# Two expert passes of 576 tokens each become one of 512 and one of 640

## The chip, the cores and the metric

The kernel runs on one core of a Trainium2 chip. The metric is the time of one execution on the device in microseconds (us), median of several runs. The core has a matrix engine (PE, with its weight loads shown as PEld), a vector engine (DVE), a scalar engine (ACT), a general one (POOL) and a queue engine (SP) that issues every transfer of this kernel. Each works through its own program in order, and the engines wait for each other by semaphores.

## The reference

Three layers follow each other: attention with pooled queries, a mixture of four experts, and a gated layer.

```python
# q, k, v: (2 batches, 8 heads, 1152, 64); queries are averaged in pairs, so 576 rows a batch
scores = scale * np.matmul(q_pool, k.transpose(0, 1, 3, 2))
attn = np.exp(scores - max); attn = attn / (attn.sum(-1) + 1e-9)
x = np.matmul(attn, v)                       # (2, 8, 576, 64), laid out as 1152 tokens x 512
...
p = domain_probs / (domain_probs.sum(-1, keepdims=True) + 1e-9)
for e in range(4):                           # w1[e]: 512 x 1024, w2[e]: 1024 x 512
    h = np.maximum(x @ w1[e], 0.0)
    out += p[:, e:e + 1] * (h @ w2[e])
...
g = out @ w_gate; val = out @ w_val          # 512 x 1536 each
return (g * sigmoid(g) * val) @ w_out        # 1152 x 512
```

## The kernel before

**Attention.** A unit is one head and one half (288) of a batch's 576 query rows, so batch 0 is units 0 to 15 and batch 1 units 16 to 31. In a unit PE makes nine blocks of scores (tile `sc`, two products each), which ACT copies to `s`; DVE takes the maximum over the blocks (`acc`); PE turns it (`mt`), DVE reduces it (`top`), PE spreads it again (`m`); DVE and POOL subtract it, ACT takes the exponential, and PE multiplies with the values (`av`). Keys and queries are turned on PE first (`tr` from `kraw` and `qraw`). At the end of a pair of units DVE inverts the sums (`den`), POOL multiplies (`xst`), and the result is split into a high part `xhi` (ACT) and a low part `xlo` (POOL or DVE): every large product is done as three products, high by high, low by high and high by low. In batch 0 the product with the values is done in plain fp32, in batch 1 in three parts too.

**Experts.** `experts(b, ...)` works on one batch of 576 tokens. Per expert it makes 8 hidden blocks of 128 and 4 output blocks of 128. Each is a group in one pair of PSUM banks: tokens 0 to 287 in one bank and 288 to 575 in the other, so a product has 288 columns (tile `ps`, line 864). Pairs `p0` and `p1` alternate. ACT and DVE take a hidden group out (`hhi`, `hlo`), DVE an output group times the probability (`yt` or `yacc`), and POOL adds it (`yacc`). Each piece of weights (128x512) comes by a transfer to `wraw`, and is split into `whi` (ACT) and `wlo` (DVE, and POOL for each second piece of the first pass). The pass of batch 0 runs among the attention of batch 1; the pass of batch 1 comes after it. The gated layer then works on all 1152 tokens, with products of 384 columns (tile `g`) and of 512 (tile `o`).

**Order.** `Plan` decides the order of everything up to the end of the first pass. Each step has a due time in units of one block of scores, an engine, a cost, and the names it reads and writes; `arrange` goes through a simple model of the engines and always takes the ready step with the earliest due time. The constants at the top (`MT`, `SUB`, `EXP`, `E0_START` and so on) are those due times. What follows the first pass is sorted by due time alone or left to the tile framework.

**Probabilities.** `prep_probs` loads the 1152x4 table (`praw`), normalizes it in seven small DVE instructions (`total`, `pn`) and stores it to memory (`pd`), from where rows are spread over the partitions (`pb`) as each expert needs them. It is one step, due at 100:

```python
at(100, "DVE", 1.0, prep_probs)
```

Of the kernel before, what the change touches and what calls it, by code (L numbers as in the profile page):

```python
# [26 lines left out]
MT, TOP, MB, MCOPY = 10.23, 11.11, 11.18, 12.05  # L27
SUB = (11.07, 10.75, 13.58)
EXP = ((13.43, 16.94, 15.82), (12.68, 14.5, 17.57))
HALF_HI = (14.41, 16.21, 16.25)  # L30
HALF_LO = (13.1, 15.0, 17.1)
AV = (17.93, 15.5)
FINISH = (22.33, 24.2)
SHARE = (0.7, 2.54, 2.4, 3.2, 3.7)
COPY, MAX = 0.94, 0.25
PREP_Q, PREP_K = (4.3, 5.58, 0.4), (6.33, -0.27)
SPLIT = (-9.69, -6)
E0_START = 159.71
E0_RATE = 9.69
# [124 lines left out]
def tile_kernel(  # L164
# [20 lines left out]
    W = 288  # L185
    NH = SQ // W
# [21 lines left out]
    hp = moe1.enter_context(tc.tile_pool(name="hp", bufs=FC1))  # L208
# [21 lines left out]
    def prep_probs():  # L230
        praw = const.tile([P, TP, NE], F32, tag="praw", name="praw")
        nc.sync.dma_start(out=praw, in_=probs.rearrange("(p t) e -> p t e", t=TP))
        total = const.tile([P, TP], F32, tag="total", name="total")
# [6 lines left out]
        nc.sync.dma_start(out=pd.rearrange("e (p t) -> p e t", t=TP), in_=pn)  # L240
# [82 lines left out]
    def take_piece():  # L323
# [9 lines left out]
        | dict(vraw=2, wraw=3, whi=2, wlo=2, hhi=FC1, hlo=FC1)  # L333
# [4 lines left out]
    xsts, xts = {}, {}  # L338
# [4 lines left out]
    def split_x(b, j, sl, hi=True, lo=True):  # L343
        if b not in xts:
            xts[b] = [
                xp.tile([P, MC, SQ], F32R, tag=f"x{n}", name=f"x{n}{b}") for n in ("hi", "lo")
            ]
        xhi, xlo = xts[b]
        src = xsts[b][:, j, sl]
        if hi:  # L350
            nc.scalar.activation(out=xhi[:, j, sl], in_=src, func=AF.Copy)
        if lo:
            eng = nc.vector if b else nc.gpsimd
            eng.tensor_tensor(
                out=xlo[:, j, sl], in0=src, in1=xhi[:, j, sl].bitcast(F32), op=ALU.subtract
            )
# [279 lines left out]
    def plan_attention():  # L636
# [55 lines left out]
        due_load_q(1, start)  # L692
        due_k(0, 0, start, "d")
        due_q(0, start, "c")
# [142 lines left out]
        for jj in range(NPAIR, B * NPAIR):  # L837
            t = 4 * KC * jj
            for i in range(2):
                ready = t + 6.7 + KC * i  # L840
# [33 lines left out]
    subs = [slice(s * W, (s + 1) * W) for s in range(NH)]  # L874

    def experts(b, at, due):

        pbs, hs, pss, yts = {}, {}, {}, {}
# [3 lines left out]
        def load_p(e):  # L882
            pbs[e] = yp.tile([P, SQ], F32, tag="pb", name=f"pb{b}_{e}", bufs=1)
            nc.sync.dma_start(
                out=pbs[e], in_=pd[e, b * SQ : (b + 1) * SQ].partition_broadcast(P)
            )

        def products(group, i, s, c, src, first, last):

            if group not in pss:  # L890
                pss[group] = pair(expert_bank(group), "ps")
# [4 lines left out]
        def expert_bank(group):  # L896
            return f"p{(group[0] * (FC1 + MC) + group[1]) % 2}"

        def two(t):
            return t.rearrange("p (s w) -> p s w", s=NH)  # L900
# [6 lines left out]
        def evict_h2(e, f):  # L907
            hl = hp.tile([P, SQ], F32R, tag="hlo", name="hlo")
            nc.vector.scalar_tensor_tensor(
                out=two(hl),  # L910
                in0=pss[e, f][:, :, :W],
                scalar=0.0,
                in1=two(hs[e, f][0]).bitcast(F32),
# [3 lines left out]
            hs[e, f].append(hl)  # L917

        def evict_y(e, o):
            if e == 0 and o == 0:  # L920
                yaccs[b] = acc.tile([P, MC, SQ], F32, tag="acc", name=f"yacc{b}")
            t = yaccs[b][:, o, :]
            if e:
                t = yts[o] = yp.tile([P, SQ], F32, tag="yt", name="yt", bufs=1)
            nc.vector.tensor_tensor(  # L925
                out=two(t), in0=pss[e, FC1 + o][:, :, :W], in1=two(pbs[e]), op=ALU.mult
            )

        def add_y(o):
            y = yaccs[b][:, o, :]  # L930
            nc.gpsimd.tensor_tensor(out=y, in0=y, in1=yts[o], op=ALU.add)  # L931

        for e in range(NE):
# [4 lines left out]
            for f in range(FC1 + 2 * MC):  # L938
                o, part = divmod(f - FC1, 2)
                hidden = f < FC1  # L940
                group = (e, f) if hidden else (e, FC1 + o)
                ps = ("ps", b, *group)
                for s in range(NH):
                    for c in range(MC):
                        if hidden:
                            src = lambda c=c: [x[:, c, :] for x in xts[b]]
                            half = s if b == 0 else 0
                            reads = [("xhi", b, c, half), ("xlo", b, c, half)]
                            uses = [("x", b)]
                            first, last = c == 0, c == MC - 1  # L950
                        else:
                            m = MC * part + c
                            src = lambda e=e, m=m: hs[e, m]
                            reads = [("hh", b, e, m), ("hl", b, e, m)]
                            uses = []
                            first, last = m == 0, m == FC1 - 1
                        at(
                            due(n), "PE", 0.397, products, group, w, s, c, src, first, last,
                            kind="r", reads=reads + [("whi", w), ("wlo", w)],
                            writes=[(*ps, s)] + ([(*ps, 1)] if first and s == 0 else []),  # L960
                            uses=uses + [ps],
                            takes=[(expert_bank(group), ps)] if first and s == 0 else [],
                        )
                        n += 3
                    if s == 0:
                        due_split(w + 1, due(n + SPLIT[0]), due(n + SPLIT[1]))
                w += 1
                if hidden:
                    at(
                        due(n - 1) + 0.35, "ACT", 0.64, evict_h, e, f,  # L970
                        reads=[(*ps, 0), (*ps, 1)], writes=[("hh", b, e, f)], uses=[ps],
                        takes=[("hhi", ("hh", b, e, f))],
                    )
                    at(
                        due(n - 1) + 0.55, "DVE", 0.75, evict_h2, e, f,
# [205 lines left out]
```

## Time and profile before

| what | us |
|---|---|
| median of 3 runs | 921.75 (921.39 to 922.65) |
| the profiled execution | 921.15 |
| its span, first to last instruction | 919.4 |
| PE busy | 884.4 |
| DVE, ACT, POOL busy | 576.6, 462.0, 388.4 |
| mean granted clock of PE | 0.997 |

The profiled execution is 0.6 us below the median, and 1.75 us of it lie outside the span. Busy time of PE is a sum of overlapping records, so a share of 96% tells only where PE is not idle. How fast it goes there is told by the distance from one product to the next.

### The profile page before, as it was taken

What the parts mean: (1) busy time and instruction counts of PE and PEld (TensorE: products, weight loads), DVE (VectorE), ACT (ScalarE), POOL (GpSimd) and SP (SyncE); (2) the same over time, 40 slices, a digit from 0 to 9 for tenths busy, and PEclk for the clock granted to TensorE, in tenths of its full rate; (3) what the DMA queues carried; (4) which work ended last, traced back from release to release, by engine and by line L of the source; (5) the groups of instructions that cost most, each with busy time, mean ns of one, the idle gap of its engine ahead of it and who ended that gap; (6) DMA issues with size and microseconds to landing.
All of it is one profiled execution on the core that took longest, in us unless ns stands there. A gap on an engine that the chain in (4) does not pass through costs nothing.

```text
span 919.4 us, 14986 instructions
## 1 busy us (share of the span) xinstructions
PE 884.4 (96%) x5916; PEld 842.3 (92%) x5916; DVE 576.6 (63%) x883; ACT 462.0 (50%) x786; POOL 388.4 (42%) x266
## 2 busy tenths in 40 slices
PE   4899998999999999999999999999999999999998
PEld 3667777899999999999999999999999999999886
DVE  4678778776667577675664334333468988888800
ACT  4678778877776767666633222232323333333110
POOL 2465657867776796778631000203023333222000
PEclk9999999999999999999999999999999999999999
DMA  5012221323233223111243232323333323223210
GB/s 141 2 41 67 49 74 39 101 71 86 72 84 92 65 73 83 46 59 60 60 148 96 89 95 81 94 88 87 92 93 99 107 70 91 92 77 98 78 69 34
DMA packets 124149, 72.30 MB, mean 79 GB/s; under 512 B 32304, under 2 KB 119344, under 8 KB 124080
## 3 DMA queue, kind: packets, MB, share of 16 engines
q1 hardware_dynamic: 124080, 71.36, 26.7%
q8 instruction: 46, 0.75, 0.3%
q14 instruction: 23, 0.19, 0.1%
HBM read 68.96 MB, written 2.38 MB: 78 GB/s over the span
## 4 chain that ended last, share of the span: by engine, by line
PE 89%; DVE 5%; ACT 3%; issue 2%; DMA 1%; POOL 1%; SPq 0%; DVEq 0%; ACTq 0%; POOLq 0%
PE ps L864 43%; PE g L864 16%; PE av L600 12%; PE o L864 8%; PE sc L494 3%; PE sc L495 3%; DVE acc L522 1%; PE mt L528 1%; ACT s L511 1%; PE tr L438 1%; PE tr L464 1%; DVE kt L456 1%; PE m L550 1%; ACT s L573 1%; DVE s L567 1%
## 5 line engine op out<-in xcount | busy, mean ns | idle before, releaser
L306 ACT ACTIVATE whi<-wraw 128x512 fp32r<-128x512 f32 x128 | 80.4, 629 | 174.6 <-PE ps L864 157.1
L567 POOL TENSOR_TENSOR s<-s,m 128x864 f32<-128x864 f32 x64 | 132.2, 2085 | 76.3 <-ACT m L560 76.2
L864 PE MATMUL ps<-xhi,whi 128*128 128x288 f32 x512 | 153.0, 299 | 0.0
L864 PE MATMUL ps<-hhi,whi 128*128 128x288 f32 x512 | 152.2, 297 | 0.0
L864 PE MATMUL ps<-hhi,wlo 128*128 128x288 f32 x512 | 151.1, 295 | 0.0
L864 PE MATMUL ps<-xhi,wlo 128*128 128x288 f32 x512 | 151.0, 295 | 0.0
L864 PE MATMUL ps<-xlo,whi 128*128 128x288 f32 x512 | 150.9, 295 | 0.0
L864 PE MATMUL ps<-hlo,whi 128*128 128x288 f32 x512 | 150.9, 295 | 0.0
L313 DVE TENSOR_TENSOR wlo<-wraw,whi 128x512 fp32r<-128x512 f32 x96 | 81.9, 853 | 101.1 <-ACT whi L306 101.1
L931 POOL TENSOR_TENSOR yacc<-yacc,yt 128x576 f32<-128x576 f32 x24 | 41.3, 1722 | 187.8 <-DVE yt L925 187.8
L511 ACT ACTIVATE s<-sc 128x576 f32<-128x576 f32 (+1 forms) x160 | 93.5, 600 | 47.6 <-PE sc L495 45.9
L573 ACT ACTIVATE s<-s 128x864 f32<-128x864 f32 x96 | 87.7, 921 | 18.4 <-DVE s L567 13.8
L864 PE MATMUL g<-yhi,wlo 128*128 128x384 f32 x288 | 96.3, 334 | 0.5 <-DVE wlo L313 0.5
L864 PE MATMUL g<-yhi,whi 128*128 128x384 f32 x288 | 96.2, 334 | 0.5 <-ACT yhi L1022 0.5
L864 PE MATMUL g<-ylo,whi 128*128 128x384 f32 x288 | 96.2, 334 | 0.0
L864 PEld LDWEIGHTS ps<-xlo,whi 128*128 128x128 f32 x512 | 96.2, 188 | 0.0
L864 PEld LDWEIGHTS ps<-hlo,whi 128*128 128x128 f32 x512 | 96.1, 188 | 0.0
L864 PEld LDWEIGHTS ps<-hhi,whi 128*128 128x128 f32 x512 | 96.1, 188 | 0.0
L864 PEld LDWEIGHTS ps<-xhi,whi 128*128 128x128 f32 x512 | 96.1, 188 | 0.0
L864 PEld LDWEIGHTS ps<-xhi,wlo 128*128 128x128 f32 x512 | 96.1, 188 | 0.0
L864 PEld LDWEIGHTS ps<-hhi,wlo 128*128 128x128 f32 x512 | 96.1, 188 | 0.0
L494 PE MATMUL sc<-qhi,kt 128*128 128x288 f32 x288 | 88.2, 322 | 4.7 <-ACT s L511 1.9
(94 smaller groups left out, 1950.7 us busy)
## 6 DMA issues: line engine op xcount, KB each, us to landing
wraw<-in_moe_w_dram SPq DMA_DIRECT2D x128, 256.0 KB, 2.7
w<-in_moe_w_gate_dram SPq DMA_DIRECT2D x12, 512.0 KB, 3.9
w<-in_moe_w_val_dram SPq DMA_DIRECT2D x12, 512.0 KB, 3.6
w<-in_moe_w_out_dram SPq DMA_DIRECT2D x12, 512.0 KB, 3.5
qraw<-in_q_dram SPq DMA_DIRECT2D x32, 144.0 KB, 2.4
kraw<-in_k_dram SPq DMA_DIRECT2D x14, 288.0 KB, 3.9
v<-in_v_dram SPq DMA_DIRECT2D x8, 288.0 KB, 4.2
vraw<-in_v_dram SPq DMA_DIRECT2D x8, 288.0 KB, 3.0
```

The lines of the kernel that those rows point to most:

```text
L306: nc.scalar.activation(out=hi, in_=t, func=AF.Copy)
L313: eng.tensor_tensor(out=lo, in0=t, in1=hi.bitcast(F32), op=ALU.subtract)
L438: nc.tensor.matmul(pt[:, m * P : (m + 1) * P], kr[:, c].rearrange("p h d -> p (h d)"), ident, is_transpose=True,)
L456: nc.vector.tensor_tensor(out=kt[other, sl], in0=pt[me, : 3 * P], in1=kt[me, sl].bitcast(F32), op=ALU.subtract)
L494: nc.tensor.matmul(ps, wt, qhi, start=True, stop=False)
L495: nc.tensor.matmul(ps, wt, qlo, start=False, stop=True)
L511: nc.scalar.activation(out=s[:, c : c + n, :], in_=ps[:, :n, :W], func=AF.Copy)
L567: eng.tensor_tensor(out=sg, in0=sg, in1=m.unsqueeze(1).to_broadcast([P, 3, W]), op=ALU.subtract)
L573: nc.scalar.activation(out=sg, in_=sg, func=AF.Exp)
L600: nc.tensor.matmul(avs[u][:, :W], w[:, c].rearrange("p t d -> p (t d)"), e, start=(c == 0 and n == 0), stop=(c == KC - 1 and n == len(term ...
L864: nc.tensor.matmul(ps, w, x, start=first and n == 0, stop=last and n == len(terms) - 1)
L931: nc.gpsimd.tensor_tensor(out=y, in0=y, in1=yts[o], op=ALU.add)
```

## The change

The experts no longer follow the batches. The first pass takes the last 512 tokens of batch 0, as single products of 512 columns. The second takes the first 64 tokens of batch 0 and all of batch 1, 640 tokens, as two products of 320 columns. So the first pass has half as many products: 768 of 512 columns where there were 1536 of 288; the second keeps 1536, of 320 columns. In the first pass a group is now two outputs, one to each bank of a pair, and taken out in one instruction of 1024 columns. The second pass has tiles of its own for the hidden part. The low and high parts of `x` lie in one tile of 640 columns, and the rows of the last layer go to their places in up to two transfers.

The work on the probabilities is three steps (load, normalize, store), placed at 100, 104 and 112. All due times of the plan have other values, and one transposition of queries is written ahead of one of keys.

```diff
-MT, TOP, MB, MCOPY = 10.23, 11.11, 11.18, 12.05
+MT, TOP, MB, MCOPY = 2.7, 9.26, 6.21, 7.32
...
-E0_START = 159.71
-E0_RATE = 9.69
+E0_START = 165.31
+E0_RATE = 9.43
...
+    T0 = 512
+    REST = SQ - T0
+    T1 = NT - T0
...
+    def load_probs():
         praw = const.tile([P, TP, NE], F32, tag="praw", name="praw")
         nc.sync.dma_start(out=praw, in_=probs.rearrange("(p t) e -> p t e", t=TP))
...
-            xhi, xlo = (x[:, subs[s]] for x in src())
-            gemm(pss[group][:, s, :W], [(whi, xhi), (whi, xlo), (wlo, xhi)], first, last)
+            xhi, xlo = src()
+            gemm(pss[group][:, s, :cols], [(whi, xhi), (whi, xlo), (wlo, xhi)], first, last)
...
-        def evict_h(e, f):
-            hh = hp.tile([P, SQ], F32R, tag="hhi", name="hhi")
-            hs[e, f] = [hh]
-            nc.scalar.activation(out=two(hh), in_=pss[e, f][:, :, :W], func=AF.Relu)
+        def evict_h(e, g):
+            hh = hp.tile([P, 2, cols], F32R, tag="hhi", name="hhi")
+            hs[e, g] = [hh]
+            nc.scalar.activation(out=hh, in_=pss[e, g][:, :, :cols], func=AF.Relu)
...
+            groups = []
+            for out in range(0, FC1 + MC, 2 - b):
+                outs = [out] if b else [out, out + 1]
+                parts = range(1 if out < FC1 else FC1 // MC)
+                groups.append([(k, part, out) for k, out in enumerate(outs) for part in parts])
...
-        at(100, "DVE", 1.0, prep_probs)
+        at(100, "SP", 0.5, load_probs, writes=[("praw",)])
+        at(104, "DVE", 1.5, prep_probs, reads=[("praw",)], writes=[("pn",)])
+        at(112, "SP", 0.5, store_probs, reads=[("pn",)])
```

What this does to the order is seen in three places. The first is SP's program at its start. Before, the load and the store of the probabilities stand between the first queries and the first keys:

```order
L421 DMA qraw_99<-in_q_dram 96x3x128 x2
L232 DMA praw<-in_moe_domain_probs_dram 128x36
L240 DMA pd<-pn 128x4x9
L370 DMA kraw_118<-in_k_dram 128x3x64 x6
L384 DMA v_102<-in_v_dram 128x9x64
```

Now the keys come second, and the probabilities stand twenty rows later:

```order
L431 DMA qraw_99<-in_q_dram 96x3x128 x2
L380 DMA kraw_106<-in_k_dram 128x3x64 x6
...
L394 DMA v_115<-in_v_dram 128x9x64
L238 DMA praw<-in_moe_domain_probs_dram 128x36
L253 DMA pd<-pn 128x4x9
L431 DMA qraw_1168<-in_q_dram 96x3x128 x2
```

The second place is PE at units 9 to 11. PE's rows are the same in both kernels from the start up to here, where two groups of the product of unit 9 (`s_895` before, `s_883` now) stand in a row. Before, the maximum of unit 10 is turned (`mt`) between the first and the second of them, and one `av` of unit 9 and two transpositions lie between its spreading (`m`) and the first `av` of unit 10 (`s_992`):

```order
L600 MATMUL av<-s_895,v_116 128x288 x3
L528 MATMUL mt<-ident,acc_1023 96x128 x3
L600 MATMUL av<-s_895,v_116 128x288 x3
L550 MATMUL m<-ident,top_1103 128x96 x3
...
L600 MATMUL av<-s_895,v_116 128x288 x3
L464 MATMUL tr<-ident,qraw_976 128x96 x3
...
L464 MATMUL tr<-ident,qraw_976 128x96 x3
...
L600 MATMUL av<-s_992,v_102 128x288 x3
```

Now both come later, after the product of unit 9, and only one pair of scores and a transposition lie between `m` and the `av` of unit 10 (`s_976`), two groups of which follow each other:

```order
L610 MATMUL av<-s_883,v_104 128x288 x3
...
L610 MATMUL av<-s_883,v_104 128x288 x3
L538 MATMUL mt<-ident,acc_1007 96x128 x3
L610 MATMUL av<-s_883,v_104 128x288 x3
L560 MATMUL m<-ident,top_1117 128x96 x3
L504 MATMUL sc<-qhi_967,kt_652 128x288
L505 MATMUL sc<-qlo_974,kt_652 128x288
L474 MATMUL tr<-ident,qraw_964 128x96 x3
L610 MATMUL av<-s_976,v_102 128x288 x6
```

What moved is the place of the maximum of a unit against the products of the unit before it. From here on the two orders differ. On DVE the seven instructions on the probabilities stand just ahead of this place, between the last maximum of unit 10 and the two `kt` that follow it.

The third place is PE where the first pass begins, after the last `av` of batch 0 (unit 15: `s_1428` before, `s_1429` now). Before, 27 products of the pass stand in a row right after one transposition:

```order
L550 MATMUL m<-ident,top_1650 128x96 x3
L600 MATMUL av<-s_1428,v_127 128x288 x6
L464 MATMUL tr<-ident,qraw_1528 128x96 x3
L864 MATMUL ps<-xhi_462,whi_1378 128x288
L864 MATMUL ps<-xlo_463,whi_1378 128x288
L864 MATMUL ps<-xhi_462,wlo_1379 128x288
```

Now the pass begins with 9 products, after one more transposition and four products of scores:

```order
L560 MATMUL m<-ident,top_1649 128x96 x3
L610 MATMUL av<-s_1429,v_115 128x288 x6
L474 MATMUL tr<-ident,qraw_1539 128x96 x3
L610 MATMUL av<-s_1429,v_115 128x288 x3
L474 MATMUL tr<-ident,qraw_1539 128x96 x3
L504 MATMUL sc<-qhi_1687,kt_1380 128x288
L505 MATMUL sc<-qlo_1691,kt_1380 128x288
...
L874 MATMUL ps<-xhi,whi_1322 128x512
L874 MATMUL ps<-xlo,whi_1322 128x512
```

Behind these 9 come one transposition, nine products `av` and four scores, and then the next 3 of the pass, which read the last quarter of `x`. By the end of the `av` of unit 17 there are 165 products of the pass on PE before and 69 now; from there on 87 a unit before and 48 now. After the last `av` of unit 31, 150 products of the first pass are left before and 30 now.

## Rows read from the trace of the kernel before

**Rows 1.** The page: busy time of each engine, and its span in 40 slices.

```profile
PE 884.4 (96%) x5916; PEld 842.3 (92%) x5916; DVE 576.6 (63%) x883; ACT 462.0 (50%) x786; POOL 388.4 (42%) x266
...
PE   4899998999999999999999999999999999999998
```

**Rows 2.** Stretches of the span: busy time of each engine, instructions in brackets.

```profile
core 0: us, PE busy (x) PEld busy (x) DVE busy (x) ACT busy (x) POOL busy (x), PEclk, DMA share, GB/s
176.35:467.24 290.89, 290.68 (x2231) 290.19 (x2230) 195.94 (x256) 201.81 (x327) 209.84 (x128) 1.00 0.25 71
467.24:690.48 223.24, 223.24 (x1687) 223.24 (x1686) 97.64 (x142) 66.58 (x111) 30.24 (x19) 1.00 0.32 96
690.48:697.34 6.86, 5.81 (x34) 5.18 (x32) 4.83 (x11) 1.37 (x3) 3.35 (x1) 1.00 0.47 151
697.34:842.02 144.68, 144.68 (x834) 144.68 (x835) 124.23 (x217) 48.61 (x95) 43.55 (x35) 1.00 0.28 88
842.02:915.50 73.48, 73.48 (x325) 60.47 (x323) 26.89 (x50) 11.99 (x20) 1.35 (x2) 1.00 0.20 65
```

**Rows 3.** Timeline of the head: start, length, engine, line, operation, tiles, idle before.

```profile
0.74 0.90 SPq L421 DMA_DIRECT2D qraw<-in_q_dram  x2
...
1.69 0.46 SPq L232 DMA_DIRECT2D praw<-in_moe_domain_probs_dram  x1
...
3.72 0.99 POOL L430 TENSOR_TENSOR qraw<-qraw 96x384 f32<-96x384 f32 x1 [0.38 <-DMA qraw<-in_q_dram]
...
3.95 0.19 DVE L234 TENSOR_REDUCE total<-praw 128x9 f32<-128x36 f32 x1 [3.95 <-DMA praw<-in_moe_domain_probs_dram]
...
5.02 0.50 DVE L239 TENSOR_TENSOR pn<-praw,total 128x9 f32<-128x9 f32 x4
...
5.55 0.39 SPq L240 DMA_DIRECT2D pd<-pn  x1
...
5.99 3.16 SPq L370 DMA_DIRECT2D kraw<-in_k_dram  x6
...
10.77 0.87 PE L438 MATMUL tr<-ident,kraw 128*128 128x128 f32 x3 [10.77 <-DMA kraw<-in_k_dram]
```

**Rows 4.** What the SP queue waited for: total, times, longest (us).

```profile
SPq L421 <- PE tr L464: 148.2, 13, 31.1
```

**Rows 5.** Timeline of PE while batch 0 is attended to.

```profile
30.50 0.43 PE L464 MATMUL tr<-ident,qraw 96*128 96x96 f32 x3
...
47.01 0.44 PE L464 MATMUL tr<-ident,qraw 96*128 96x96 f32 x3
...
48.59 3.18 PE L600 MATMUL av<-s,v 128*128 128x288 f32 x12 [1.15 <-ACT s L573]
...
67.22 0.47 PE L464 MATMUL tr<-ident,qraw 96*128 96x96 f32 x3
...
116.12 0.51 PE L528 MATMUL mt<-ident,acc 128*96 128x128 f32 x3
...
171.51 1.62 PE L600 MATMUL av<-s,v 128*128 128x288 f32 x6
...
172.97 0.41 PE L550 MATMUL m<-ident,top 96*128 96x96 f32 x3
...
176.35 0.38 PE L864 MATMUL ps<-xhi,whi 128*128 128x288 f32 x1
```

**Rows 6.** Timeline of POOL and ACT where the first expert pass begins.

```profile
182.32 0.84 POOL L632 TENSOR_TENSOR xst<-num,den 128x288 f32<-128x288 f32 x1
...
184.34 0.45 ACT L351 ACTIVATE xhi<-xst 128x288 fp32r<-128x288 f32 x1
...
185.10 0.83 POOL L354 TENSOR_TENSOR xlo<-xst,xhi 128x288 fp32r<-128x288 f32 x1
```

**Rows 7.** Groups by line and shape: busy us, mean ns of one.

```profile
L905 ACT ACTIVATE hhi<-ps 128x576 fp32r<-128x576 f32 x64 | 40.7, 636 | 0.1
...
L909 DVE SCALAR_TENSOR_TENSOR hlo<-ps,hhi 128x576 fp32r<-128x576 f32 x64 | 48.1, 752 | 12.0 <-ACT hhi L905 11.8
```

**Rows 8.** Timeline where the second expert pass begins.

```profile
467.28 0.41 ACT L619 ACTIVATE num<-av 64x288 f32<-64x288 f32 x1 [2.68 <-PE av L600]
...
473.30 0.75 DVE L354 TENSOR_TENSOR xlo<-xst,xhi 128x576 fp32r<-128x576 f32 x1
```

**Rows 9.** Timeline of PE where the gated layer begins.

```profile
691.52 0.45 PE L864 MATMUL g<-yhi,wlo 128*128 128x384 f32 x1 [0.54 <-DVE wlo L313]
...
697.34 0.62 PE L864 MATMUL g<-yhi,whi 128*128 128x384 f32 x2 [0.51 <-ACT yhi L1022]
```

More of the change, by code (lines that the diff above doesn't have):

```diff
@@ L343, in split_x @@
     def split_x(b, j, sl, hi=True, lo=True):
[L344 to L348, printed above, removed]
+        if not xts:
+            xts[:] = [xp.tile([P, MC, T1], F32R, tag=f"x{n}", name=f"x{n}") for n in ("hi", "lo")]
+        shift = b * REST
+        xhi, xlo = (x[:, j, sl.start + shift : sl.stop + shift] for x in xts)
         src = xsts[b][:, j, sl]
         if hi:
-            nc.scalar.activation(out=xhi[:, j, sl], in_=src, func=AF.Copy)
+            nc.scalar.activation(out=xhi, in_=src, func=AF.Copy)
         if lo:
             eng = nc.vector if b else nc.gpsimd
-            eng.tensor_tensor(
-                out=xlo[:, j, sl], in0=src, in1=xhi[:, j, sl].bitcast(F32), op=ALU.subtract
-            )
+            eng.tensor_tensor(out=xlo, in0=src, in1=xhi.bitcast(F32), op=ALU.subtract)
     def where(u):
@@ L873, in tile_kernel, with tokens, experts @@
     yaccs = {}
-    subs = [slice(s * W, (s + 1) * W) for s in range(NH)]
-    def experts(b, at, due):
+    def tokens(b, table, e):
+        row = table[e]
+        return [row[REST:SQ]] if b == 0 else [row[:REST], row[SQ:]]
+    def experts(b, at, due, pool):
+        N = T1 if b else T0
+        cols = N // 2 if b else N
         pbs, hs, pss, yts = {}, {}, {}, {}
@@ L937, in experts @@
             )
[L938 to L968, printed above, removed]
-                    at(
-                        due(n - 1) + 0.35, "ACT", 0.64, evict_h, e, f,
-                        reads=[(*ps, 0), (*ps, 1)], writes=[("hh", b, e, f)], uses=[ps],
-                        takes=[("hhi", ("hh", b, e, f))],
-                    )
-                    at(
-                        due(n - 1) + 0.55, "DVE", 0.75, evict_h2, e, f,
-                        reads=[(*ps, 0), (*ps, 1), ("hh", b, e, f)], writes=[("hl", b, e, f)],
-                        uses=[ps], takes=[("hlo", ("hl", b, e, f))],
-                    )
-                elif part == 1:
-                    y = ("yt", b, e, o) if e else ("y", b, o)
-                    at(
-                        due(n - 1) + 0.35, "DVE", 0.755, evict_y, e, o,
-                        reads=[(*ps, 0), (*ps, 1), ("pb", b, e)], writes=[y], uses=[ps],
-                        takes=[("yt", y)] if e else [("acc", ("yacc", b))] if o == 0 else [],
-                    )
-                    if e:
-                        at(
-                            due(n - 1) + 0.7, "POOL", 1.45, add_y, o, kind="port",
-                            reads=[y], writes=[("y", b, o)],
-                        )
@@ L1008, in due_split, with rows @@
             due_load(i + 3, t2)
+    def rows(p):
+        parts = []
+        for start, end, t in ((0, T0, REST), (T0, SQ, 0), (SQ, NT, SQ)):
+            lo, hi = max(p, start), min(p + P, end)
+            if lo < hi:
+                parts.append((lo - p, hi - p, t + lo - start))
+        return parts
     def gated():
```

165 lines of the change are left out of this document (119 added, 46 removed).

## The prediction

> **What bounds the kernel now.** I read the page first, then the stretches of the span, then timelines at the places that the new order touches. PE is busy 96% of the span, no other engine above 63%; over the 40 slices only the first is below 8 tenths [rows 1]. The stretches tell the two regimes apart [rows 2]. Up to 176.35 us PE attends to batch 0. From there to 467.24 it mixes the attention of batch 1 with the first expert pass, and is idle for 0.2 us of 290.89. From 467.24 to 690.48 it does nothing but expert products, without a gap, and then the gated layer with one gap of about 1 us. So from 176.35 on the end moves only with what PE itself has to do, or if the change makes PE wait. Before that, PE waits: 10.77 us for the first keys [rows 3], and then in short pieces, such as 1.15 us for an exponential [rows 5]. The granted clock is 1.00, the level of 2.4 GHz, in all five stretches [rows 2], so I expect none of the difference from it.
>
> What a product costs there is its distance to the next, not its busy record. Of 288 columns: 223.24 / 1686 = 132.4 ns. Of 384: 144.68 / 834 = 173.5 ns. Of 512, in the last stretch with its 324 products: 73.48 / 324 = 226.8 ns [rows 2]. At 2.4 GHz the columns alone are 120, 160 and 213.3 ns, so each product carries 12 to 14 ns that do not depend on its width. No row shows 320 columns; on the line from 288 to 384 they cost 146.1 ns, on that from 288 to 512 145.9 ns. I take 146.1.
>
> **The change part by part.** All sums are against the profiled execution, 921.15 us, 0.6 below the median.
>
> *Products.* Both kernels push 884,736 columns through the experts; the change has 768 products fewer. Before: 3072 x 0.1324 = 406.7 us, 203.4 in each pass. Now the first pass is 768 x 0.2268 = 174.2 (29.2 less) and the second 1536 x 0.1461 = 224.4 (21.0 more). Together 398.6: **-8.1 us**. With 145.9 ns for 320 and 226.1 (73.48 over all 325 records) for 512 it is -9.0, with some missing records the other way -7.9. The saving is the difference of a gain inside the attention of batch 1 and a loss behind it; the loss is certain, the gain needs PE to stay gapless there.
>
> The row of 512 columns has a fixed part of 13.5 ns and that of 288 one of 12.4 [rows 2]. The Trainium skill (TensorE: Matmul & The Clock Gate, section Back-to-back issue gap) gives the gap of a warm single product as N/2.4 + 2.5 ns; by that the 768 products fewer would save 2.0 us, and the end would be 6 us later than my sum. The same section gives 131 ns for 512 columns in a sustained stream, which this trace contradicts with 226.8. I go by the rows.
>
> *The head.* SP issues the first keys at 5.99 us, held back by the store of `pn` at 5.55, which waits for the load of the table (landed 3.95) and for DVE's `pn` at 5.02 to 5.52 [rows 3]. Now the keys come right behind the two loads of the first queries, whose issue takes from 0.74 to 1.64; where the table's load is issued now, at 1.69 [rows 3]. PE's first transposition of keys and all rows of PE up to the `mt` of unit 10 are the same in both orders, so the shift carries down the chain: 5.99 - 1.69 = **-4.3 us**. It can be less: the queries' own packets are in flight until about 3.7 (POOL starts on them at 3.72), and if the keys then land no earlier than if issued at 3.7, it is -2.3. At most -5.3 (a choice), if the table's transfers also got in their way. The work that was in the head comes back on DVE at units 10 and 11: seven instructions, from 3.95 to 5.52, 1.6 us [rows 3], ahead of two copies of keys that PE needs only in the next pair of units; I cost it at nothing, and at 1.6 if that cover is gone. The store waits on SP for `pn`, and behind it stands a load of queries, which waits anyhow for the transpositions of the tile before it, in 13 waits 148.2 us in all [rows 4].
>
> *The order of units 10 to 15.* The new order delays the `mt` and `m` of some units behind the product of the unit before, and leaves no `av` between `m` and the next exponential. In a pair of units before, one spot of this kind cost 1.15 us [rows 5]. I pieced the new order together from stretches of before. From the `mt` at 116.12, the rest of the product of unit 9 with scores and turning is about 4.2 us (to 120.3). Then two kinds of stretches follow: from transposition to transposition of queries 47.01 to 67.22 is 20.2, and 30.50 to 47.01 is 16.5 [rows 5]. To each I add one group of three `av`, 172.97 - 171.51 = 1.46 us [rows 5], for the second `av` that no longer lies under the wait: 120.3 + 21.7 + 18.0 + 20.2 = 180.2. With the transposition and four scores that now stand ahead of the first product (0.8) it starts at 181.0 instead of 176.35: **+4.6 us**. The 0.8 is work taken from later: **-0.8**. Bounds of the net 3.8: 0, if these stretches cost no more than before, and 8, if each of the five units waits 1.5 us more.
>
> *The start of the first pass.* Products 10 and on read the last quarter of `x`, unit 15's output. Before, its `xst` began at 182.32, `xhi` at 184.34 and `xlo` ended at 185.93 [rows 6], 13.0 us after the last `m` at 172.97 [rows 5]; but 27 products needing only the first half stood ahead. Now 9 stand there. From `m` to the first product was 176.35 - 172.97 = 3.4; three more `av` (1.46) and the 0.8 above lie in it now; then the 9 products (2.0) and, ahead of the tenth, a transposition, nine `av` and four scores (about 2.0, at 132.4 ns a product). PE is there 9.7 us after `m`, and 13.0 - 9.7 leaves a wait: **+3.3**. Bounds: 0, if POOL, which has other rows ahead of `xst`, makes it earlier by as much, and 4.8, if the product of unit 15, now 1.46 us longer behind `m`, delays the whole chain.
>
> *The gated layer's start.* PE waits 0.54 us there for `wlo` and 0.51 for `yhi` [rows 9]. The last output is now 320 wide instead of 576 and its chain shorter: **-0.5**, bounds -1.05 and +1, if the split of rows over two transfers costs what it saves.
>
> *Costed at nothing.* The takings-out of a hidden group are 636 ns on ACT and 752 on DVE for 576 columns [rows 7]; for 1024, by width, 1.13 and 1.34, together 2.5 us against the 24 x 0.2268 = 5.4 us of the next group that hides them. At the junction of the passes, the chain from the last `av` at 467.24 to the last `xlo`, ending at 474.05, takes 6.8 us [rows 8]; before it hid under 150 products (19.9 us), now under 30 of the first pass and 9 of the second, 30 x 0.2268 + 9 x 0.146 = 8.1. Cover remains by 1.3 us; if ACT or DVE come to it late by more, PE waits for the excess.
>
> **Sum:** -8.1 - 4.3 + 4.6 - 0.8 + 3.3 - 0.5 = -5.8: 915.35 for the profiled execution, 916.0 for the median.
>
> **The rivals.** *Orders cost nothing.* The pieced stretches and the 3.3 us of the start are my construction; PE had waits in 0.2 us of 290.89 only, and one place may lose what the next had as slack. Then -8.1 - 4.3 - 0.5 = -12.9: 908.9.
>
> *Order eats the gain.* The order at its bound of 8 and the start at 4.8: -8.1 - 4.3 + 8 + 4.8 - 0.5 = -0.1: 921.7, no difference that can be told (this kernel's measurement resolves about 0.2%, 1.8 us). For it: five units in a row have the new pattern. Against it: an equal bound at each is more than the 1.15 us seen.
>
> *Attention of batch 1 cannot go faster* (the other side). From 176.35 to 467.24 a unit takes 290.89 / 16 = 18.2 us. PE's work without the 1386 products there is 290.89 - 183.5 = 107.4; with 738 of 512 columns it is 107.4 + 167.4 - 0.8 = 274.0, or 17.1 a unit. POOL, at 209.84 of 290.89 (72%) [rows 2], would be at 77%, and the chain `mt`, `top`, `m`, subtraction, exponential has less of PE's work to hide under. If the units stay at 18.2, the 29.2 is not earned but the 21.0 is paid: 290.89 + 30 x 0.2268 + 224.4 = 522.1 against 514.1, +8.0; with -4.3 + 4.6 - 0.5 the sum is +7.8: 929.6. It decides from a loss of 5.8 / 16 = 0.4 us a unit on, and the result is slower from there. Against it: PE waits nowhere in this stretch now, and no engine but PE is above 72%.
>
> **How the numbers follow.** Forecast 0.52, orders cost nothing 0.23, order eats the gain 0.10, attention cannot go faster 0.15. The forecast's own range is 911 to 919.9. For 8 in 10 I go down past 908.9 and up to 922, which holds most of the rival at 921.7, and leave out the last one with the outer ends: 906.5 to 922. Faster 0.75 (the first two), same 0.10, slower 0.15.
>
> **What would show it.** The first transposition of keys at about 6.5 instead of 10.77; the first expert product at about 176.7 (176.35 - 4.3 + 4.6); a gap of PE of about 3 us some 4 us behind the ninth product; 227 ns a product in the first pass and 146 in the second, where it runs alone; PE idle under 1 us between there and the end of the attention. Wrong would make it: keys that land no earlier; PE idle by tenths of a microsecond in every unit of batch 1, with POOL or ACT named as what ended it; a wait for `xlo` between the passes; a product of 320 columns that costs more than the line through its neighbours.

## The result and the profile after

The changed kernel takes 932.65 us (931.87 to 933.31, 4 runs), the kernel before 921.58 (921.39 to 922.65) beside it: a ratio of 1.0115, interval 1.0102 to 1.0128. It is slower by 1.2%, where 916.0 was forecast, and lies above the range of 906.5 to 922.

One sentence on the change ahead of the prediction was too wide: only the hidden groups are taken out in one instruction of 1024 columns. The outputs are taken out one by one, as `evict_y(e, g, o, s)` in the diff says: the first output of a pair (in the second pass, the first half of an output) while PE still makes the other in the other bank of the same tile. Most of what follows hangs on this.

The page of the changed kernel, its busy times and PE's 40 slices, to be held against [rows 1]:

```profile
PE 889.0 (96%) x5148; PEld 806.4 (87%) x5148; DVE 579.5 (62%) x883; ACT 461.4 (50%) x770; POOL 390.3 (42%) x278
...
PE   5898889989999999999999999999999999999998
```

The totals tell nothing: PE has 768 instructions fewer and is 4.6 us longer busy. The stretches of the changed kernel do, cut at the first expert product, the last `av` and the first `g`, with the columns of [rows 2]:

```profile
0.00:176.52 176.52, 151.55 (x823) 121.56 (x824) 128.52 (x211) 131.69 (x235) 101.68 (x84) 0.98 0.25 63
176.52:461.21 284.69, 278.46 (x1574) 241.98 (x1572) 196.15 (x243) 200.40 (x312) 212.06 (x131) 1.00 0.27 76
461.21:702.70 241.49, 234.34 (x1569) 231.22 (x1567) 101.06 (x157) 66.11 (x108) 31.04 (x27) 1.00 0.30 88
702.70:927.30 224.60, 224.60 (x1189) 211.62 (x1188) 153.76 (x274) 62.64 (x116) 45.52 (x37) 0.99 0.25 80
```

Against the four stretches of before (176.35, 290.89, 223.24 and 225.02) this is +0.2, -6.2, +18.3 and -0.4. The forecast by the same cuts was +0.3, -13.6, +8.0 and -0.5. So two stretches missed: the attention of batch 1 by 7.4 us, and what comes between its end and the gated layer by 10.3. In both PE now idles, 6.2 and 7.2 us, where before it idled 0.2 and 0. What PE waited for from 176 to 703 us, by group (us in all, times, longest):

```profile
PE ps L874 <- DVE yt L944: 5.9, 5, 1.9
PE ps L874 <- DVE hlo L926: 2.6, 4, 0.8
PE ps L874 <- DVE wlo L326: 2.3, 2, 1.2
PE mt L538 <- DVE acc L529: 1.2, 1, 1.2
PE ps L874 <- ACT s L521: 0.6, 1, 0.6
PE ps L874 <- DVE yacc L944: 0.5, 1, 0.5
```

DVE is busy 62% of the time, and yet it ends most of these waits. That points to a dependence rather than to a lack of DVE; the runs below test it. Three of the waits on PE's timeline, one in the first pass, one where the second expert begins in the second pass, and one before the gated layer:

```profile
303.53 0.50 PE L874 MATMUL ps<-hhi,whi 128*128 128x512 f32 x1 [0.78 <-DVE yt L944]
...
531.13 0.38 PE L874 MATMUL ps<-xhi,whi 128*128 128x320 f32 x1 [0.81 <-DVE hlo L926]
...
700.91 0.42 PE L874 MATMUL ps<-hhi,whi 128*128 128x320 f32 x1 [1.86 <-DVE yt L944]
```

The first and the third stand in the middle of a group: three products into the second bank of its tile have already run, and no new tile is opened there. In the first pass, the first output is taken out only behind those three products of the second output, and PE goes on only behind that:

```profile
302.36 0.39 PE L874 MATMUL ps<-hhi,wlo 128*128 128x512 f32 x1
...
302.78 0.69 DVE L944 TENSOR_TENSOR yt<-ps,pb 128x512 f32<-128x512 f32 x1 [0.67 <-PE ps L874]
```

The program's order on PE shows why (an output of the second pass, `ps_5003`, with the semaphores that are waited for):

```
2335 L874 MATMUL ps_5003<-hhi_4902,whi73_4994 128x320
...
2338 L874 MATMUL ps_5070<-hhi_4759,whi74_5029 128x320 [waits Activation_49]
...
2361 L874 MATMUL ps_5070<-hhi_4867,wlo74_5030 128x320
2362 L874 MATMUL ps_5003<-hhi_4937,whi73_4994 128x320 [waits DVE_49]
```

The first three products of the last piece of the second half are written ahead of the first half's taking-out; the other nine come behind it in the program and wait for DVE. The framework, which orders the second pass itself, has put 24 products of the next output (2338 to 2361) in between. At the last output of an expert, these 24 belong to a hidden group of the next expert; then DVE has `wlo` and that group's `hlo` ahead of the last taking-out, and PE waits until that `hlo` is done:

```profile
529.55 0.69 DVE L326 TENSOR_TENSOR wlo<-wraw,whi 128x512 fp32r<-128x512 f32 x1 [3.54 <-ACT whi L319]
530.16 0.82 DVE L926 SCALAR_TENSOR_TENSOR hlo<-ps,hhi 128x640 fp32r<-128x640 f32 x1
530.90 0.48 DVE L944 TENSOR_TENSOR yacc<-ps,pb 128x320 f32<-128x320 f32 x1
```

In the first pass, whose order is written out, nothing can be put in between, and PE waits in place.

**Theory A:** a product into one bank waits for DVE reading the other bank, because both lie in one tile and the framework sets the waits by tiles. **Theory B** (the rivals): DVE's row is late for reasons of its own, the width of 320, or an attention that cannot go faster; the waits would only move.

### The profile page after: what moved, and what is told of

Its sections match the earlier page's. It is cut to its first block, busy times and chain, and to the rows that moved or that the text cites. A ratio compares the mean times of both kernels' runs of the same rounds, so it can differ in the third digit from the quotient of the medians.

```text
span 930.8 us, 13450 instructions
## 1 busy us (share of the span) xinstructions
PE 889.0 (96%) x5148; PEld 806.4 (87%) x5148; DVE 579.5 (62%) x883; ACT 461.4 (50%) x770; POOL 390.3 (42%) x278
## 4 chain that ended last, share of the span: by engine, by line
PE 84%; DVE 6%; ACT 4%; POOL 2%; issue 2%; DMA 1%; SPq 0%; DVEq 0%; ACTq 0%; POOLq 0%
PE ps L874 40%; PE g L874 16%; PE av L610 11%; PE o L874 8%; PE sc L504 3%; PE sc L505 3%; ACT s L521 2%; DVE acc L532 2%; POOL s L577 1%; ACT s L583 1%; PE mt L538 1%; PE tr L448 1%; PE tr L474 1%; ACT kt L464 1%; DVE kt L466 1%
## 5 line engine op out<-in xcount | busy, mean ns | idle before, releaser
L874 PE MATMUL ps<-hhi,whi 128*128 128x320 f32 (+1 forms) x384 | 131.0, 341 | 7.0 <-DVE yt L944 5.9
L874 PE MATMUL ps<-xhi,whi 128*128 128x320 f32 (+1 forms) x384 | 131.0, 341 | 2.6 <-DVE hlo L926 2.6
L874 PE MATMUL ps<-hhi,wlo 128*128 128x320 f32 (+1 forms) x384 | 129.6, 338 | 1.1 <-DVE wlo L326 1.1
L874 PE MATMUL ps<-xhi,wlo 128*128 128x320 f32 (+1 forms) x384 | 128.9, 337 | 1.2 <-DVE wlo L326 1.2
L874 PE MATMUL ps<-hlo,whi 128*128 128x320 f32 (+1 forms) x384 | 129.4, 337 | 0.0
L874 PE MATMUL ps<-xlo,whi 128*128 128x320 f32 (+1 forms) x384 | 129.3, 337 | 0.0
L583 ACT ACTIVATE s<-s 128x864 f32<-128x864 f32 x96 | 87.8, 921 | 10.8 <-DVE s L577 8.2
L1115 POOL TENSOR_TENSOR gl<-g,gh 128x384 fp32r<-128x384 f32 x36 | 44.6, 1239 | 106.8 <-ACT gh L1114 106.8
L610 PE MATMUL av<-s,v 128*128 128x288 f32 x288 | 80.1, 420 | 3.2 <-ACT s L583 3.2
L505 PE MATMUL sc<-qlo,kt 128*128 128x288 f32 x288 | 81.5, 299 | 0.0
L595 POOL TENSOR_TENSOR el<-s,eh 128x864 fp32r<-128x864 f32 x32 | 67.0, 2095 | 27.5 <-ACT eh L588 27.5
```

Source lines behind the costliest of these rows:

```text
L505: nc.tensor.matmul(ps, wt, qlo, start=False, stop=True)
L583: nc.scalar.activation(out=sg, in_=sg, func=AF.Exp)
L595: eng.tensor_tensor(out=lo, in0=src, in1=parts[u, g][0].bitcast(F32), op=ALU.subtract)
L610: nc.tensor.matmul(avs[u][:, :W], w[:, c].rearrange("p t d -> p (t d)"), e, start=(c == 0 and n == 0), stop=(c == KC - 1 and n == len(term ...
L874: nc.tensor.matmul(ps, w, x, start=first and n == 0, stop=last and n == len(terms) - 1)
L1115: nc.gpsimd.tensor_tensor(out=gl[:, sl], in0=g, in1=gh[:, sl].bitcast(F32), op=ALU.subtract)
```

## The experiments

The times of the kernel before beside them are 921.1 to 921.5; "a tail" is the stretch from the last `av` to the first `g`.

**1 and 2. Taking out after the group.** The edit gathers the outputs of a group and takes them out when the last is made, in the second pass alone or in both:

```diff
-                            o = out - FC1
-                            at(due(n - 1) + 0.35, "DVE", 0.69, evict_y, e, g, o, s, ...)
+                            done.append((out - FC1, s))
+                            if b not in LATE_OUT or len(done) == 2:
+                                for i, (o, s) in enumerate(done):
+                                    at(due(n - 1) + 0.35 + 0.7 * i, "DVE", 0.69, evict_y, ...)
```

> The changed kernel (932.65 us), with the two halves of an output of the second pass taken out one behind the other after the last product of the group, instead of the first half in the middle of the second half's products. Theory A (a product into one bank waits for the taking-out of the other bank, because both lie in one tile; in the second pass that pushes nine products behind the next piece): the three waits of 0.81 at the start of an expert and the one of 1.86 before the end go, with what PE takes to restart after each, about 5 us: 927.6 (926.5 to 929). The nine products stand behind their group again. Theory B (the waits come from DVE being late with its own row of work, and only move): 931.5 to 933.5, with waits of the same size at the next taking-out.

Measured: 924.61 us (922.96 to 925.66), ratio 1.0029 (1.0019 to 1.0038). 8.0 us gone, more than A said; 7.6 of it lies behind the first expert product in the profiled executions. The order is straight; what PE still waited for in its tail:

```profile
PE ps L875 <- DVE yt L945: 1.6, 1, 1.6
PE ps L875 <- DVE hlo L927: 0.5, 1, 0.5
```

The tail fell from 241.49 to 235.08, and the gated layer by 1.1 more: in the changed kernel the waits ahead of it left the clock at 0.76 from 702.70 to 708, with the waits gone it stays full.

> The same in both passes: in the first pass too, the first output of a pair is taken out only after the last product of the second. Theory A: the waits for yt and yacc in the first pass (0.52, 0.78, 0.85, 0.78, 1.57, together 4.5, with restarts about 5.5) go as well: about 5 below the kernel with the second pass alone, 922.5 (921 to 925). Theory B: DVE takes out two outputs in a row, and the second waits for POOL's addition, so that DVE is late for the attention: 927 to 931, with new waits of PE for the maximum or the subtraction.

Measured: 924.82 us (923.82 to 926.05). Nothing more, but it tells neither theory apart: the plan starts an instruction as soon as its model has the engine free, so a later due time did not move the taking-out, and PE's waits in the first pass are those of the changed kernel:

```profile
PE ps L875 <- DVE yt L945: 4.0, 4, 1.6
...
PE ps L875 <- DVE yacc L945: 0.5, 1, 0.5
```

**3. The same, enforced in the plan.** The taking-out names both banks as read, so that the plan cannot start it before the second output is made: `reads=[(*ps, 0), (*ps, 1), ("pb", b, e)]`.

> Taking out after the last product of the group, in both passes, now enforced in the first pass by making the first output's taking-out read both banks in the plan (in the run before, the plan's model started it early as DVE was free, and the order of the first pass stayed as it was). Theory A (the waits for yt and yacc in the middle of a second output are those of one tile for two banks): 4.5 of idle PE in the first pass goes, with restarts about 5, so 919.6 against 924.6 with the second pass alone (918.5 to 921). Theory B (two takings-out in a row make DVE late for the attention, or POOL's addition holds the second): 923.5 to 926, with waits for maxima or for the next pair of banks.

Measured: 918.53 us (917.55 to 919.89), ratio 0.9976 (0.9966 to 0.9985). Another 6.1 us, a little more than A's 5. No `yacc` or `yt` stands among PE's waits within the first pass any more (one of 0.5 for `yt` is left where the second pass begins), and attention goes through in 279.84 us against 284.69 (the two stretches up to and behind the last `av`):

```profile
175.68:455.52 279.84, 276.67 (x1574) 242.00 (x1572) 196.36 (x243) 199.97 (x312) 212.54 (x131) 1.00 0.27 77
455.52:688.67 233.15, 232.59 (x1569) 230.93 (x1567) 104.47 (x155) 66.12 (x107) 29.56 (x26) 1.00 0.30 91
```

**4. The cost put into the kernel before.** 288 columns and all else as before, but the halves of an output of the second pass are taken out one by one, the first right behind its last product.

```diff
+                    if b and part == 1 and not hidden:
+                        at(due(n - 1) + 0.35, "DVE", 0.45, evict_y, e, o, s, ...)
```

> The kernel before (921.1), with one thing of the change put in: in the second pass the two halves of an output are taken out one by one, the first right after its last product, while the second half is still being made in the other bank of the same tile. 288 columns as before, and nothing else changed. Theory A (that is what makes the waits of the changed kernel's second pass): three waits of about 0.8 at the start of an expert, nine products pushed behind the next piece, a wait of nearly 2 at the end, and the time longer by 6 to 8 us, 927 to 929. Theory B (the waits of the changed kernel come from the width of 320 or from its new hidden tiles): within 1 us of 921.1, no such waits.

Measured: 928.82 us (928.08 to 930.74), ratio 1.0089 (1.0071 to 1.0107): 7.5 slower, as A said. PE's order now has 24 products of the next output ahead of the last nine, as in the changed kernel. The waits that this tail did not have before:

```profile
PE ps L864 <- DVE hlo L909: 2.6, 3, 0.9
PE ps L864 <- DVE yt L926: 2.5, 1, 2.5
PE ps L864 <- DVE wlo L313: 0.4, 1, 0.4
```

Neither the width of 320 nor the new hidden tiles are needed for them.

**5. The tile or the moment.** The halves of the second pass are taken out as early as in the changed kernel, but lie in tiles of one bank each:

```diff
-                pss[group] = pair(f"p{group[1] % 2}", "ps")
+                if b and group[1] >= FC1:
+                    n = (2 * group[1] + s) % 4
+                    pss[group, s] = (single("cd"[n], "ps") if n < 2
+                        else pair(("p2", "p1")[n - 2], "ps")[:, 0])
```

> The changed kernel (932.65) with the outputs of the second pass in tiles of one bank each, in four different places that the attention has left free; each half is still taken out right after its last product, as in the changed kernel. Theory A (PE waits because both halves lie in one tile, not because the taking-out is early or behind others on DVE): the order is straight again, the waits for hlo and yt in the second pass go, and the time falls as much as with the late taking-out, by about 8: 924.0 to 925.5. Theory B (it is the early taking-out's place in DVE's row): 930 or more.

Measured: 923.69 us (923.06 to 924.4), ratio 1.0023 (1.0012 to 1.0034). 9.0 us gone with the taking-out where it was. In the second pass no wait is left; the one of its tail is that of the first pass's last output, which still lies in a pair:

```profile
PE ps L874 <- DVE yt L953: 1.6, 1, 1.6
```

So in the second pass the early moment costs nothing without the shared tile. The four places also are more room than the two pairs, which this run does not keep apart from the tile; run 1, which keeps the pairs and moves the moment, gains nearly as much without more room. In the first pass only the moment was moved (run 3).

**6 and 7. The head.** The kernel before with the probabilities as three steps, at the change's places and then at 120, 124 and 132:

```diff
-        at(100, "DVE", 1.0, prep_probs)
+        at(100, "SP", 0.5, load_probs, writes=[("praw",)])
+        at(104, "DVE", 1.5, prep_probs, reads=[("praw",)], writes=[("pn",)])
+        at(112, "SP", 0.5, store_probs, reads=[("pn",)])
```

> The kernel before with one part of the change: load, normalization and store of the probabilities as three steps at 100, 104 and 112, so that the keys come second on SP. Theory A (the first keys come 5.8 us earlier, as the changed kernel's first transposition at 4.99 instead of 10.77 shows, and the whole chain moves with them): 915.8 to 917.0. Theory B (batch 0 is held by something else later on, and the head's gain is lost there, as the first expert product at 176.52 in the changed kernel could be read): 920.5 to 922.

Measured: 920.67 us (919.92 to 921.45), ratio 0.9990 (0.9980 to 1.0001): no difference, as B said. The first transposition is at 4.63, but the first expert product only at 174.93.

> The kernel before with only the probabilities moved, to 120, 124 and 132. PE's order is that of the kernel before throughout batch 0. Theory A (the head gives 5.8, and only the reordering at 100 lost it): 915.5 (914.8 to 916.8). Theory B (batch 0 is bounded by something that does not move with the keys): 919.5 to 921.5.

Measured: 915.81 us (915.35 to 916.87), ratio 0.9948 (0.9933 to 0.9962), as A said. With its first keys' transposition at 4.81 the first expert product is at 170.62 instead of 176.35 [rows 5]. So the head is worth 5.3 us, and the place of the normalization took most of it back. From the first transposition to the first expert product it is 165.6 us in the kernel before and 165.8 here, but 170.3 in run 6 and 171.5 in the changed kernel, 0.8 of it for four scores and a transposition more. (Runs 1, 2, 3 and 5 have the changed kernel's program there and took 170.0 to 172.6: one execution does not tell a microsecond.)

What this time goes into is only in part a wait. At units 9 to 11 of the changed kernel DVE has the seven instructions on the probabilities, one of them with 0.92 us, and PE's order is another. PE waits 1.52 us ahead of a transposition, for which the profile names no releaser; the program has it wait for DVE's subtraction `s` of unit 10, which ends 0.1 us ahead of it. Then it waits 0.47 for an exponential, and its clock goes from the upper level to the lower one (timeline, and stretches with the clock in the third column from the end):

```profile
114.90 0.30 PE L505 MATMUL sc<-qlo,kt 128*128 128x288 f32 x1
...
115.56 1.05 DVE L577 TENSOR_TENSOR s<-s,m 128x864 f32<-128x864 f32 x1
...
116.72 0.44 PE L474 MATMUL tr<-ident,qraw 96*128 96x96 f32 x3 [1.52 <-issue]
117.63 2.74 PE L610 MATMUL av<-s,v 128*128 128x288 f32 x6 [0.47 <-ACT s L583]
```

```profile
116.00:118.00 2.00, 0.81 (x5) 0.60 (x6) 2.00 (x3) 1.35 (x3) 2.00 (x2) 1.00 0.00 0
118.00:122.00 4.00, 4.00 (x11) 2.88 (x10) 1.63 (x4) 1.94 (x3) 3.03 (x3) 0.57 0.00 0
```

At the lower level the products of `av` follow each other at 0.48 us instead of 0.24. That costs about 1.5: in run 1, with the same program and the same two waits there, the clock stays full, and the stretch is 1.5 shorter. But the kernel before has waits of this kind as well: from 97 us behind the first transposition on, PE idles 6.1 us there and 7.0 in the changed kernel. The rest, two to three microseconds, is spread: in the new order PE's products follow each other more slowly (`av` at 248 ns on average in run 1 against 237 in run 7, from 100 us behind the first transposition on, waits left out). Why they do is not shown.

**8. The due times of before** at the top of the changed kernel.

> The changed kernel with all due times (the table at the top) of the kernel before. Theory A (the new due times cost about 6 us in batch 0, which is why the first expert product stands at 176.52 although the head gained 5.8): the first expert product at about 170.7 and the time at about 926.5 to 928 if the rest stays. Theory B (the new due times fit the new passes, and those of before make the first pass wait): first product at 170.7 or so, but 931 or more in all, with longer waits in the attention of batch 1.

Measured: 940.4 us (938.49 to 941.81), ratio 1.0194 (1.0176 to 1.0211). B in the time. The first product is at 175.41, not the 170.7 of both theories: the table is not what slows batch 0. What the old table does is to use up the first pass too early: no product of it is left after the last `av`, the second pass begins at once, and the chain to the last quarter of `x` lies open:

```profile
478.75 0.42 PE L874 MATMUL ps<-xhi,whi 128*128 128x320 f32 x1 [3.91 <-ACT xhi L363]
```

With the 0.55 for `xlo` behind it that is 4.5 of the 7.8 us; PE also idles 1.7 more among the attention of batch 1.

**9 and 10. The probabilities at 120 in the changed kernel**, with the late taking-out in the second pass, and in both.

> The kernel with the late taking-out in the second pass (924.6), with the three steps on the probabilities placed at 120, 124 and 132 instead of 100, 104 and 112. PE's order in batch 0 is then that of the kernel before up to unit 12. Theory A (the place of the normalization reorders units 9 to 12 on PE, PE waits there, its clock falls to half for four microseconds, and 4.5 of the head's gain is lost in it): 920.1 (919 to 921.5), first expert product at about 170.5. Theory B (the loss is in units 13 to 15, whose order differs from the kernel before for other reasons): 923.5 to 925, first product at 174 to 176.

Measured: 923.02 us (921.5 to 924.99), ratio 1.0022 (1.0012 to 1.0031). Between the theories: the first product is at 169.84 as A said, 5.2 earlier, but only 1.6 us remain of it at the end.

> Both of these together. If they are independent, as theory A says of each: about 915.2, below the kernel before (921.3). If one hides the other, or theory B holds for either: 919 to 924.

Measured: 916.98 us (916.75 to 918.64), ratio 0.9963 (0.9948 to 0.9977). 1.6 below run 3 again, and between the 915.2 and the 919 of the expectation. The stretch from the first expert product to the last `av` is 5.2 longer than in run 3, so what was given back lies in there; the longest wait stands where the pass begins. DVE and POOL there:

```profile
182.42 5.62 DVE L327 TENSOR_TENSOR wlo<-wraw,whi 128x512 fp32r<-128x512 f32 x1 [0.57 <-ACT whi L320]
```

```profile
180.22 2.06 POOL L578 TENSOR_TENSOR s<-s,m 128x864 f32<-128x864 f32 x1
182.22 2.04 POOL L596 TENSOR_TENSOR el<-s,eh 128x864 fp32r<-128x864 f32 x1
184.19 2.07 POOL L578 TENSOR_TENSOR s<-s,m 128x864 f32<-128x864 f32 x1
186.20 1.29 POOL L327 TENSOR_TENSOR wlo<-wraw,whi 128x512 fp32r<-128x512 f32 x1
```

An instruction that takes 0.69 us where nothing disturbs it takes 5.62, as long as POOL works without a gap; PE waits 2.12 for it, and its clock is at the lower level from 188.9 to 192.3. The changed kernel has the same at 185.91 (4.55 us, beside 4.05 of `s` on POOL), and PE's wait of 1.17 ends with it. In the kernel before none of these instructions takes more than 2.2.

**11 and 12. That piece on POOL.**

```diff
-        on_pool = i < PER_BATCH and i % 2
+        on_pool = i < PER_BATCH and (i % 2 or i == 2)
```

> The kernel with the late taking-out in both passes and the probabilities at 120 (916.98), with the low part of the third piece of weights (number 2) made on POOL instead of DVE. In that kernel DVE's instruction for it took 5.62 us instead of 0.69, from 182.42 on, while POOL ran four instructions on SBUF without a gap, and PE waited 2.12 and 1.36 right there. Theory A (DVE was blocked by POOL for as long as POOL's instructions followed each other; in POOL's own row the work cannot be blocked so): the wait of 2.12 shrinks, and about 3 of the 5 us that the earlier start of batch 0's end gained but gave back here are kept: 913.5 to 915. Theory B (the start of the pass is held by POOL's and ACT's amount of work, not by the blocking): 916.5 to 918.5, with PE waiting for POOL instead.

Measured: 915.59 us (915.48 to 915.89), ratio 0.9940 (0.9924 to 0.9955). It tells neither theory apart: the plan counted the instruction on POOL, but `split_lo` chooses the engine by a condition of its own, and it stayed on DVE (3.96 us there). With the same edit in `split_lo` too:

> In the run before this one the edit reached only the plan's cost: the instruction for the low part of piece 2 stayed on DVE, began 1.8 us later, was blocked for 3.27 us instead of 4.93, and the time fell by 1.4. Here it really is on POOL, between two of POOL's own instructions, everything else as in that run. Theory A (blocking of DVE by POOL's unbroken row): it ends at about 185.7 instead of 188.2, no DVE instruction on two SBUF operands lies beside POOL's row there, the wait of 1.85 goes, with the clock at full level behind it: 912.5 to 914.5. Theory B (POOL's row gets longer by 1.3 and the attention waits for it): 915 to 917, with PE waiting for el or s on POOL.

Measured: 912.99 us (910.56 to 913.45), ratio 0.9904 (0.9886 to 0.9921). A: 2.6 below run 11, whose plan is the same, and the clock stays full here. POOL has it at 185.69, and DVE's instructions beside it have their usual lengths:

```profile
185.69 1.29 POOL L327 TENSOR_TENSOR wlo<-wraw,whi 128x512 fp32r<-128x512 f32 x1
```

```profile
184.89 0.76 DVE L533 TENSOR_TENSOR acc<-sc,acc 128x576 f32<-128x576 f32 x1
185.68 0.56 DVE L467 TENSOR_TENSOR kt<-tr,kt 64x384 fp32r<-64x384 f32 x1
186.45 1.23 DVE L927 SCALAR_TENSOR_TENSOR hlo<-ps,hhi 128x1024 fp32r<-128x1024 f32 x1 [0.21 <-ACT hhi L923]
```

This is the fastest version: the new split of tokens, outputs taken out behind their group, the probabilities at 120 and one more piece on POOL. Most of its gain is not the split's: the kernel before with only the probabilities at 120 (run 7) takes 915.81, 1.2 less than the split with late taking-out (run 10) and 2.8 more than this.

## Why the prediction was wrong

The step that failed is the one headed "Costed at nothing". It priced the taking-out by the width of the hidden groups, 2.5 us under 5.4 of the next group, and gave the outputs no price of their own, as if they were taken out like a hidden group. It asked how long the taking-out lasts, not what has to wait for it in the program. That was missed in the diff (`s` among the arguments of `evict_y`) and in the order of the changed program, which shows nine products pushed behind 24. Its price: 8.0 us in the second pass and 6.1 in the first, 14.1 of the 16.6 between 916.0 and 932.65. Term by term (us; the measured ones from profiled executions):

| term | forecast | measured |
|---|---|---|
| taking-out of outputs (runs 1 and 3, behind the first expert product) | 0 | +14.2 |
| expert products (run 3) | -8.1 | -5.8 |
| head, at the first transposition | -4.3 | -5.8 |
| order of units 10 to 15, less the work taken from later | +4.6 - 0.8 | +5.9 - 0.8 |
| start of the first pass | +3.3 | +2.5 |
| PE's other products among the attention of batch 1 (run 3) | 0 | +2.1 |
| gated layer, with the clock full (run 3) | -0.5 | -1.5 |
| sum | -5.8 | +10.8 |

Between the profiled executions lie 11.5; the remaining 0.7 is in no term.

*Products, -8.1.* The mechanism was right, the size too large. With the waits gone (run 3) all expert products together take 405.4 us from start to start, without idle time, against 411.3 before: -5.8. The 1536 products of 320 columns run at 147.1 ns on average, where the line through the neighbours gave 146.1; those of 512 columns among the attention at 230.5 behind another one of their kind (run 12), and at about 316 behind a transposition, against 226.8 alone [rows 2]. PE's other products there, put at nothing, also run further apart: 103.9 us in run 3 against 102.6, though 0.8 of them had moved ahead. By the formula of the Trainium skill that was weighed against the rows (TensorE: Matmul & The Clock Gate, section Back-to-back issue gap), an estimate for 320 columns is 135.8 ns and for the saving 1.9 us (2.0 in the prediction); no run comes near that gap, 147.1 is measured.

*The head, -4.3.* Right in mechanism, too small: 5.8 at PE's first product, 5.3 of the time in run 7.

*The order of units 10 to 15, +4.6 less 0.8.* From the first transposition to the first expert product it cost 5.9 in the changed kernel. That this product stands at 176.52, where the prediction had 176.7, is luck: head and order were both too small, by 1.5 and 1.3. The cause given, waits for exponentials in each unit, was wrong in the main: PE idles only 0.9 more, the lower clock costs about 1.5, and the rest is products that follow each other more slowly. And it comes from the place of the probabilities, not from the due times: with them at 120 it is gone in both kernels (runs 7 and 9), with the old due times it stays (run 8).

*The start of the first pass, +3.3.* PE waited 2.5, so the size was about right, but by accident: nothing waits ahead of the tenth product, and no product waits for `xlo`. The waits come at 190.52 and 194.93, for `wlo` and for a maximum, both behind the DVE instruction of 4.55 us.

*The junction, at nothing.* The cover of 8.1 us held for the chain to `xlo`: no wait for it. Run 8 shows what it costs without cover: 3.9 for `xhi`, and 0.55 for `xlo` behind it.

*The gated layer, -0.5.* -0.4, but as a sum: the two waits of [rows 9] are gone, and with the clock full from the start it is about -1.5 (run 3); in the changed kernel the clock, at the lower level from 701.9 to 705.3, took the difference.

*The rival "attention cannot go faster"* came nearest in time (929.6), by the wrong mechanism: the stretch goes through in 279.84 us with POOL busy 212.54 of it, when the taking-out does not hold PE.

## What to carry to other kernels

Where two results share a tile and one is taken out while the other is made, the second one's products may have to wait for it, and a framework that orders by itself may hide that by moving other work ahead: look at the order for products that have gone behind work which they used to precede. A step that is moved off an idle engine at the start is not free where it lands; try two or three places. And a fixed order of due times belongs to the widths for which it was made.

## What was not expected of the hardware

DVE's 128x512 subtraction of two SBUF operands took 3.96 to 5.62 us instead of 0.69 beside an unbroken row on POOL (runs 11 and 10, and 4.55 in the changed kernel), over two or three POOL instructions; a maximum that reads one operand from PSUM kept its 0.76 beside POOL (run 12). The Trainium skill (SBUF — State Buffer, section SBUF: two separate sides) says that DVE with two SBUF inputs and POOL exclude each other from a shared pair of ports, each for the whole of an instruction. The trace agrees, and goes further: DVE was kept out over several POOL instructions in a row. That moving one piece to POOL gave 2.6 us (915.59 to 912.99, with the same plan) fits it; the lock itself no run shows.
